# Attention and two mixture layers on one core: a planner's durations, its order, and 30 extra matmuls ahead of the first scores

## The chip, the cores and the metric

One core of a Trainium2 chip runs the whole program. The metric is device time in microseconds (us), median of several runs.

## The reference

Inputs: `q`, `k`, `v` of shape (2, 8, 768, 64), 16 centroids for each head, and the weights of two feed-forward layers. What is computed:

```python
q_assign = argmax(einsum('bhsd,hcd->bhsc', normed(q), normed(centroids)), -1)   # k_assign the same from k
mask = q_assign[:, :, :, None] == k_assign[:, :, None, :]
scores = where(mask, q @ k.T / sqrt(D), -1e9)
x = softmax(scores) @ v                       # (2, 8, 768, 64), then laid out as (1536, 512)
h = x @ w_in;  x = (h * clip(h + 3, 0, 6) / 6) @ w_out          # first layer, 512 -> 2048 -> 512
p = domain_probs / domain_probs.sum(-1)
out = sum(p[:, e] * (relu(x @ w1[e]) @ w2[e]) for e in range(4))  # second layer, 512 -> 1024 -> 512 each
```

## The kernel before, in words

The work is done batch by batch. For batch 0 the program runs attention (`Attn`, its block function is `turned`), then the first layer (`Moe1`), then the second (`Moe2`); attention of batch 1 (block function `block`) is mixed in between the matmuls of batch 0's two layers, and the two layers of batch 1 come last.

Attention goes by pairs of heads (four pairs, `hp`) and blocks of 256 queries (three, `blk`): twelve units in a batch, each of four score tiles (two heads, 128 queries each). `prep` loads the raw heads (`raw`), makes `qa` and `ka` on ScalarE and `kb` and parts of `qa` on VectorE or GpSimd, and gets the cluster of each token: centroid scores on TensorE (`psc`, after the normed centroids were transposed into `cps` and copied to `ct`), a copy `sc`, a transpose `psct`, a chain on VectorE (`mx`, `cs`, `oh` or, for the first pair, `ohq`), and a transpose back (`pso`) that is copied into rows 64 to 80 of `kb` and `qb`. A score tile (`pss`) is two matmul pairs; VectorE takes its maximum (`ut`), ScalarE its exponential (`e`), GpSimd scales it (L752), TensorE transposes it (`pst`), ScalarE or VectorE copies that to `pt`, and the value matmuls (`psv`) follow; ScalarE and VectorE make the float16 halves `x1h` and `x1l` of the result. In batch 1 the transposes are DMAs (`pt<-p`).

While attention of batch 0 runs, `conv_w` turns weights, which are handed in as float64 words, to float32: a load `r64` (a ring of three buffers, L971), ScalarE (L974), GpSimd (L975), three operations on VectorE (L977, L979, L981), a square sum on ScalarE (L983), then two float16 halves that go to DRAM (`hl_i`, `hl_o`) and are read back as `w`. In the layers, products of two float32 matrices are three matmuls of float16 halves (`mm3`, L994 to L996). `post` of `Moe1` takes a finished tile (`psg`): ScalarE (`t`, L1141), VectorE (`t`, L1142), ScalarE and VectorE (`g`, L1143 and L1144). The four tiles of `Moe1`'s first chunk and first token block share one PSUM buffer (L1124), so that each waits for L1142 of the tile before.

No engine's order is written by hand. Every operation is added to an `Order` as a task with an engine, a duration and a priority; `plan` lays the tasks out by list scheduling with these durations, and `emit` issues them in that order. On the chip each engine then works through its own list in order, each instruction waiting on semaphores. The table `PAR` holds the priorities' parameters. The helpers `act`, `dve` and `pool` in `body` turn a tile's width into a duration for the planner; they emit nothing by it.

Of the kernel before, what the change touches and what calls it, by code (L numbers as in the profile page):

```python
# [9 lines left out]
F32 = mybir.dt.float32  # L10
# [4 lines left out]
AF = mybir.ActivationFunctionType  # L15
# [12 lines left out]
def _f32(u):  # L28
# [11 lines left out]
    thr=3060,  # L40
    off=0.0,
    wsl="DD",
    wx=-7.066418236159021,
    wxs=1.7031729906943276,
    wx0=60.44894795273649,
    wl=5.8905461872446105,
    slack=0.05,
    nl=0.5,
    vre=2,
    nbv=12.208119445812287,  # L50
    nbr=19.492100909063655,
    xw=[4.0, 8.0],
    pw=(1, 1),
    prl=10.307879853622739,
    q0=-100.0,
    q1=4.698832831216272,
    psc="ms",
    ql=6,
    ahead=2.5,
    wait=0,  # L60
    wait0=0.8,
    until=15.937819815454496,
    wgap=4,
    ta=23.03227176398944,
    tu=2.65261639137209,
    lead0=24.89126820071733,
    lead2=1.9834016944625252,
    vlead2=-8.255446311119922,
    lead1=2.584304629357875,
    vlead=-26.23423839669475,  # L70
    avp=-2.177772012892397,
    parts=3,
    avpa=-5.181945553955072,
    kn='PPPPPD',
    kt='AAADA',
    kb='DPAD',
    gl=["DDDD", "DDDD"],
    mx=33.765926285870314,
    sp=12.85212467284476,
    spc=-0.7733117880477255,  # L80
    wse=dict(i="P", o="S", **{"1": "P", "2": "A"}),
    v0=49.64382789476431,
    lr=0.3,
    spm=1.5,
    pem=0.0,
    v1=-30.274294106096814,
# [3 lines left out]
    loa="VP",  # L90
    lob="VV",
    r64p=10.082714135814108,
    slow=1.127922433051184,
    psx=3,
    dup=["PSSS", "P"],
    dpx=2,
    trp=5.40052463189909,
    trh=2,
    parta=6,
    cv0=136.29846708597177,  # L100
    cvd=12.748195272086846,
    cva=2,
    cvb=(3, 8, 4),
    wo1=0,
# [4 lines left out]
    wr=8,  # L109
    wob=8,  # L110
    two=[0, 0],
    seq=[0, 1, 3, 2, 5, 4, 6, 7, 9, 10, 8, 11],
    btail=8.42579664942202,
    bu0=37.05195126419793,
    bdu=25.500617255218906,
    bvl=-6.574407994641807,
    bpr=5.123744591407974,
)


# [267 lines left out]
def body(ctx: ExitStack, tc: tile.TileContext, qk, vd, cent, w_in, w_out, probs, w1, w2, out):  # L388
    nc = tc.nc
    B, H, _, S = qk.shape  # L390
# [18 lines left out]
    G = PAR  # L409
    o = Order(tc)  # L410
    add = o.add

    def pe(n, prio, fn, r, w, cols=0):
        return add("PE", n, prio, fn, r, w, cols=cols or 2400 * n)

    def act(n, prio, fn, r, w, ps=False, ap=0, acc=False, tab=None, lag=0.0):
        return add("ACT", 1e-3 * (n * 0.8325 + (93 if ps else 129) + 93 * ap + 93 * acc), prio, fn, r, w, tab=tab, lag=lag)

    def dve(n, prio, fn, r, w, fast=False, ap=False, lag=0.0, lk=False):
        return add("DVE", 1e-3 * (n / (1.92 if fast else 0.96) + 68 + 60 * ap), prio, fn, r, w, lag=lag, lk=lk or fast)  # L420

    def pool(n, prio, fn, r, w, ns=2.1):
        return add("POOL", 1e-3 * (n * ns + 150), prio, fn, r, w, lk=True)

    def dma(nbytes, prio, fn, r, w, lag=0.0, start=0.0):
# [149 lines left out]
    class Attn:  # L575
# [16 lines left out]
        def prep(self, hp, p, lo_eng):  # L592
# [5 lines left out]
            for q in range(2):  # L598
                h = 2 * hp + q
                raw = self.buf("raw", [128, S], F32)  # L600
                dma(393e3, p(0), lambda raw=raw, h=h: nc.sync.dma_start(out=raw.t, in_=qk[b, h]), [], [raw])
                qa, qb, ka, kb = (self.buf(k, [n, S], F32R) for k, n in (("qa", 128), ("qb", 80), ("ka", 128), ("kb", 80)))
                heads.append((qa, qb, ka, kb))
                raws.append(raw)
                act(S, p(1), lambda qa=qa, raw=raw: nc.scalar.activation(out=qa[0:64], in_=raw[0:64], func=AF.Copy, scale=0.125), [raw], [(qa, 0)])
                dma(196e3, p(1), lambda qa=qa, qb=qb: nc.sync.dma_start(out=qb[0:64].bitcast(F32), in_=qa[0:64].bitcast(F32)),
                    [(qa, 0)], [(qb, 0)])

                def low(eng, f, r, w, at=2, n=S):
                    if eng == "V":  # L610
                        dve(n, p(at), lambda: f(nc.vector), r, w, lk=True)
                    else:
                        pool(n, p(at), lambda: f(nc.gpsimd), r, w)

                def keys(qa=qa, ka=ka, kb=kb, raw=raw, after=[sc] if quick and q else [], kl=G["ql"] if quick and q else 0):
                    act(S, p(1), lambda: nc.scalar.activation(out=ka[64:128], in_=raw[64:128], func=AF.Copy), [raw] + after, [(ka, 1)])
# [14 lines left out]
                if quick and q:  # L631
                    late = keys
                else:
                    keys()
# [66 lines left out]

            pe(6 * 0.054, p(5), otr, [oh], [po])
            so = self.buf("so", [64, S], F32R)
            act(S, p(5), lambda: nc.scalar.activation(out=so.t, in_=po.t, func=AF.Identity, scale=ohs.t, bias=ohb.t), [po], [so], ps=True, ap=True)
# [133 lines left out]
        def scores(self, qa, qb, ka, kb, q0, tb, n, p):  # L838
            ps = Buf(p_s[self.b], [128, 2, 512], F32, "pss")

            def score():
# [10 lines left out]
            dve(S, p, lambda: nc.vector.tensor_reduce(out=nb(), in_=ps[:, :, 0:HS], axis=AX.XY, op=ALU.max, negate=True), [ps], [(tb, n)])  # L852
            act(S, p, lambda: nc.scalar.activation(  # L853
                out=e.t.rearrange("p (a b) -> p a b", a=2), in_=ps[:, :, 0:HS], func=AF.Exp, bias=nb(), scale=1.0, accum_out=rs()),
                [ps, (tb, n)], [e, (tb, 2 + n)], ps=True, acc=True, tab=AF.Exp)
            return e

        def sums(self, tb, n, p, unit=1.0 / PSC):
# [552 lines left out]
```

## Time and profile before

| what | value |
|---|---|
| median of 3 runs | 957.32 us (956.35 to 958.79) |
| the profiled execution's own time | 955.95 us |
| its span, first to last instruction | 954.1 us |
| instructions | 16183 |
| TensorE (PE) busy | 918.0 us, 96% of the span |
| VectorE (DVE) busy | 722.6 us, 76% |
| ScalarE (ACT) busy | 648.0 us, 68% |
| GpSimd (POOL) busy | 369.4 us, 39% |

Busy time of an engine is the union of its instructions' times. A matmul's time runs from its first row in to its last row out, and the next one starts before that, so TensorE's share is high even where its pace is not. The 1.85 us between the span and the execution's own time lie outside the instructions.

### The profile page before, as it was taken

The numbers are of one execution on the slowest core, as the hardware profiler recorded it, in microseconds if no ns is written. First come the engines' busy times: TensorE is split into PE (matmuls) and PEld (weight loads), VectorE is DVE, ScalarE is ACT, GpSimd is POOL, SyncE is SP. The second block draws the span as 40 slices with busy tenths as digits, with TensorE's granted clock in tenths as the row PEclk, the third lists the DMA queues.
The fourth block names the chain that finished last, engine by engine and source line by source line (L and its number), as shares of the span: only waits on it lengthen the run. The fifth ranks groups of instructions, "written<-read, shape, count | busy, mean of one in ns | idle before, by whom it ended". The sixth has DMA issues, their size and how long they took to land. (4 is left out here: it accounts for less than half of the span.)

```text
span 954.1 us, 16183 instructions
## 1 busy us (share of the span) xinstructions
PE 918.0 (96%) x5633; PEld 545.6 (57%) x5633; DVE 722.6 (76%) x1513; ACT 648.0 (68%) x1360; POOL 369.4 (39%) x406
## 2 busy tenths in 40 slices
PE   5998998999999998999999999999999999999998
PEld 3776765655555554555565565566655555555553
DVE  8899785887679997798798987855589666564543
ACT  5899986767788787879787754565467654555411
POOL 3566735424535435635455321101132552334100
PEclk9999999999999999999999999999999999999999
DMA  7343339776535475277576677332021221212001
GB/s 228 109 142 98 132 109 323 275 257 218 177 99 180 95 173 150 68 154 167 129 128 145 181 164 219 108 108 91 23 79 46 99 88 46 89 55 79 0 1 67
DMA packets 124369, 121.63 MB, mean 127 GB/s; under 512 B 81472, under 2 KB 81472, under 8 KB 124288
## 3 DMA queue, kind: packets, MB, share of 16 engines
q1 hardware_dynamic: 124288, 120.61, 44.1%
q8 instruction: 44, 0.72, 0.3%
q14 instruction: 37, 0.30, 0.1%
HBM read 81.32 MB, written 14.68 MB: 101 GB/s over the span
## 5 line engine op out<-in xcount | busy, mean ns | idle before, releaser
L900 POOL TENSOR_TENSOR w<-wraw,w 128x512 f16<-128x512 f32 (+1 forms) x128 | 133.9, 1062 | 191.7 <-ACT w L899 147.7
L994 PE MATMUL psm<-w,h 128*128 128x512 f16 x384 | 145.9, 380 | 0.1
L996 PE MATMUL psm<-w,h 128*128 128x512 f16 x384 | 145.5, 379 | 0.0
L995 PE MATMUL psm<-w,h 128*128 128x512 f16 x384 | 145.5, 379 | 0.0
L853 ACT ACTIVATE e<-pss,ut 128x768 f32<-128x768 f32 x96 | 86.6, 903 | 19.2 <-DVE ut L852 14.7
L852 DVE TENSOR_REDUCE ut<-pss 128x1 f32<-128x768 f32 x96 | 91.1, 950 | 8.7 <-PE pss L846 8.1
L1081 ACT ACTIVATE keep<-psw 128x384 f32<-128x384 f32 x96 | 46.6, 487 | 67.9 <-PE psw L1073 67.7
L898 POOL TENSOR_SCALAR wraw<-wraw,wsc 128x512 f32<-128x512 f32 x64 | 47.5, 751 | 94.5 <-DMA wraw<-in_w 43.4
L899 ACT ACTIVATE w<-wraw 128x512 f16<-128x512 f32 (+1 forms) x128 | 72.2, 581 | 17.3 <-POOL wraw L898 6.6
L995 PE MATMUL psg<-g,w 128*128 128x384 f16 x256 | 83.4, 326 | 0.3 <-DVE g L1144 0.3
L994 PE MATMUL psg<-g,w 128*128 128x384 f16 x256 | 83.5, 326 | 0.0
L996 PE MATMUL psg<-g,w 128*128 128x384 f16 x256 | 83.4, 326 | 0.0
L1258 DVE SCALAR_TENSOR_TENSOR oa<-psm,pq,oa 128x512 f32<-128x512 f32 x84 | 61.9, 744 | 22.7 <-PE psm L996 22.5
L995 PEld LDWEIGHTS <-w 128*128 128x128 f16 x512 | 50.1, 98 | 39.2 <-issue 8.1
L996 PEld LDWEIGHTS <-w 128*128 128x128 f16 x512 | 50.0, 98 | 35.6 <-issue 2.5
L994 PEld LDWEIGHTS <-w 128*128 128x128 f16 x512 | 51.0, 100 | 33.9 <-issue 1.4
L1234 DVE SCALAR_TENSOR_TENSOR h<-psw,h 128x384 f16<-128x384 f32 x78 | 43.1, 553 | 31.3 <-ACT h L1233 31.0
L844 PE MATMUL pss<-ka,qa 128*128 128x384 f32 x192 | 61.3, 401 | 4.9 <-ACT e L853 4.5
L1071 PE MATMUL psw<-tx,ws 128*128 128x384 f16 x192 | 62.6, 326 | 1.1 <-DVE h L1234 0.8
L996 PEld LDWEIGHTS <-h 128*128 128x128 f16 x384 | 37.6, 98 | 45.3
L1073 PE MATMUL psw<-tx,ws 128*128 128x384 f16 x192 | 62.6, 326 | 0.0
L1072 PE MATMUL psw<-tx,ws 128*128 128x384 f16 x192 | 62.6, 326 | 0.0
(199 smaller groups left out, 2367.5 us busy)
## 6 DMA issues: line engine op xcount, KB each, us to landing
wraw<-in_w SPq DMA_DIRECT2D x128, 256.0 KB, 3.3
r<-in_w_in SPq DMA_DIRECT2D x16, 512.0 KB, 4.8
r<-in_w_out SPq DMA_DIRECT2D x16, 512.0 KB, 4.9
w<-hl_i SPq DMA_DIRECT2D x32, 256.0 KB, 2.8
w<-hl_o SPq DMA_DIRECT2D x32, 256.0 KB, 4.1
raw<-in_qk SPq DMA_DIRECT2D x16, 384.0 KB, 4.1
vr<-in_vd SPq DMA_DIRECT2D x12, 384.0 KB, 4.9
hl_i<-w SPq DMA_DIRECT2D x16, 256.0 KB, 3.5
```

The source lines that it names most:

```text
L844: nc.tensor.matmul(ps[:, f, 0:HS], qa[:, qs], ka[:, f * HS:f * HS + HS], start=True, stop=False)
L852: dve(S, p, lambda: nc.vector.tensor_reduce(out=nb(), in_=ps[:, :, 0:HS], axis=AX.XY, op=ALU.max, negate=True), [ps], [(tb, n)])
L853: act(S, p, lambda: nc.scalar.activation(out=e.t.rearrange("p (a b) -> p a b", a=2), in_=ps[:, :, 0:HS], func=AF.Exp, bias=nb(), scale=1.0 ...
L899: act(c, p, lambda w=w, raw=raw, c=c: nc.scalar.activation(out=w[:, 0, 0:c], in_=raw[:, 0:c], func=AF.Copy), [raw], [(w, 0)])
L900: pool(c, p, lambda w=w, raw=raw, c=c: nc.gpsimd.tensor_tensor(out=w[:, 1, 0:c], in0=raw[:, 0:c], in1=w[:, 0, 0:c], op=ALU.subtract), [raw ...
L994: nc.tensor.matmul(o_, ah, bh, start=i == 0, stop=False)
L995: nc.tensor.matmul(o_, ah, bl, start=False, stop=False)
L996: nc.tensor.matmul(o_, al, bh, start=False, stop=i == 3)
L1071: nc.tensor.matmul(o_, ah, bh, start=not more and k == 0, stop=False, skip_group_check=more)
L1072: nc.tensor.matmul(o_, ah, bl, start=False, stop=False, skip_group_check=more)
L1073: nc.tensor.matmul(o_, al, bh, start=False, stop=k == 1, skip_group_check=more)
L1258: dve(512, p, lambda: nc.vector.scalar_tensor_tensor(out=oa[:, t], in0=ps.t, scalar=q, in1=oa[:, t], op0=ALU.mult, op1=ALU.add), [ps, qk], ...
```

## The change

Three things change in the file. The planner's duration formulas get other constants (`act`, `dve`, `pool`, and the widths given for a few tasks). The table `PAR` gets other priorities, among them `seq`, the order of the twelve units of batch 0, in which a unit is the number `3 * hp + blk`. And 30 tasks are added for TensorE: a plain matmul of the float32 identity by itself, 128 by 128, into a PSUM tile `spin` that nothing reads.

```diff
-    seq=[0, 1, 3, 2, 5, 4, 6, 7, 9, 10, 8, 11],
+    seq=[1, 0, 3, 2, 5, 4, 6, 7, 9, 10, 11, 8],
...
+    warm=30,
+    wat=2.2,
+    wstep=0.5,
...
-    kn='PPPPPD',
+    kn='PPPPDD',
...
     def act(n, prio, fn, r, w, ps=False, ap=0, acc=False, tab=None, lag=0.0):
-        return add("ACT", 1e-3 * (n * 0.8325 + (93 if ps else 129) + 93 * ap + 93 * acc), prio, fn, r, w, tab=tab, lag=lag)
+        return add("ACT", 1e-3 * (n * 0.8325 + (62 if ps else 104) + 85 * ap + 118 * acc), prio, fn, r, w, tab=tab, lag=lag)
...
-        return add("DVE", 1e-3 * (n / (1.92 if fast else 0.96) + 68 + 60 * ap), prio, fn, r, w, lag=lag, lk=lk or fast)
-
-    def pool(n, prio, fn, r, w, ns=2.1):
+        return add("DVE", 1e-3 * (n / (1.92 if fast else 0.96) + 68 + 60 * ap + 52 * (lk or fast)), prio, fn, r, w, lag=lag, lk=lk or fast)
+
+    def pool(n, prio, fn, r, w, ns=1.92):
...
+    spin = Buf(p_v[0], [128, 128], F32, "spin")
+    for i in range(G["warm"]):
+        w = pe(0.2133, 900.0 if i else -200.0, lambda: nc.tensor.matmul(spin.t, ident.t, ident.t, start=True, stop=True), [], [spin], 512)
+        w.ready = G["wat"] + G["wstep"] * i
```

Engine by engine, the program after holds the same instructions in the same numbers as the program before, and the 30 matmuls; all else is a matter of order. Three places follow, as the two programs list them. In the changed file lines stand three further down (seven further from L1276 on), so L646 of before is L649 of after.

The first place is the head of TensorE's list, from its first matmul to the first transpose of one-hot codes (`ohq`). Before:

```order
L537 MATMUL cps<-ident,scrap 128x128
L646 MATMUL psc<-raw,ct 32x384 x4
L656 MATMUL psct<-ident,sc 128x128 x3
L683 LDWEIGHTS ohq
L683 MATMUL pso<-ident_b,ohq 128x128
```

And after:

```order
L1276 MATMUL spin<-ident 128x128 x5
L540 MATMUL cps<-ident,scrap 128x128
L1276 MATMUL spin<-ident 128x128 x2
L649 MATMUL psc<-raw,ct 32x384 x4
L1276 MATMUL spin<-ident 128x128 x4
L659 MATMUL psct<-ident,sc 128x128 x3
L1276 MATMUL spin<-ident 128x128 x11
L686 LDWEIGHTS ohq
L686 MATMUL pso<-ident_b,ohq 128x128
```

Of the 30 matmuls 22 stand here, around the centroid scores and their transposes; four more stand behind the twelve `pso` transposes, ahead of the first score, and the last four behind the second pair's centroid scores, two score tiles later.

The second place is TensorE's list between the last score tile of the third unit of batch 0 (first row) and that unit's value matmuls (last row); the rows between are later scores (`pss`), transposes (`pst`) and the value matmuls of the unit before. Before:

```order
L846 MATMUL pss<-kb,qb 128x384 x2
L780 MATMUL psv<-pt,vr 64x256 x12
L764 MATMUL pst<-ident,e 128x128 x6
L844 MATMUL pss<-ka,qa 128x384 x2
L846 MATMUL pss<-kb,qb 128x384 x2
L764 MATMUL pst<-ident,e 128x128 x6
...
L846 MATMUL pss<-kb,qb 128x384 x2
L764 MATMUL pst<-ident,e 128x128 x3
L780 MATMUL psv<-pt,vr 64x256 x12
```

And after:

```order
L849 MATMUL pss<-kb,qb 128x384 x2
L767 MATMUL pst<-ident,e 128x128 x3
L847 MATMUL pss<-ka,qa 128x384 x2
L849 MATMUL pss<-kb,qb 128x384 x2
L767 MATMUL pst<-ident,e 128x128 x3
...
L849 MATMUL pss<-kb,qb 128x384 x2
L767 MATMUL pst<-ident,e 128x128 x3
L783 MATMUL psv<-pt,vr 64x256 x12
```

The 12 value matmuls of the unit before no longer stand between, and of `pst` transposes 21 stand there in place of 27; four later score tiles stand there in both, and six small `pso` transposes come in.

The third place is ScalarE's list at the end of attention of batch 0, with buffer numbers: `x1h0` of the last unit, the loads' first step (`wconv<-r64`), and `post`'s first step of the third tile of `Moe1` (`psg1_2039` before, `psg1_2077` after). Before:

```order
L788 ACTIVATE x1h0_602<-psv_1981,vm_66 128x256
L974 ACTIVATE wconv_2049<-r64_1977 128x512
L974 ACTIVATE wconv_2063<-r64_1991 128x512
L1141 ACTIVATE t_2066<-psg1_2039,hlf_76,kt_69 128x384
L1143 ACTIVATE g_2074<-t_2066 128x384
```

And after:

```order
L977 ACTIVATE wconv_2038<-r64_1999 128x512
L791 ACTIVATE x1h0_637<-psv_2015,vm_66 128x256
L986 ACTIVATE scrap_77,am_2023<-wconv_2008 128x512
L1144 ACTIVATE t_2102<-psg1_2077,hlf_76,kt_69 128x384
L977 ACTIVATE wconv_2108<-r64_2036 128x512
```

The first of the two loads' steps now stands ahead of `x1h0`, the second behind the tile's `t`. On the DMA queue the load of `r64_2036` now stands ahead of four read-backs `w<-hl_o`, where its like of before, the next `r64` load, stood behind them.

## Rows read from the trace of the kernel before

**Rows 1.** The page: span, busy time by engine, the granted clock in 40 slices.
```profile
span 954.1 us, 16183 instructions
PE 918.0 (96%) x5633; PEld 545.6 (57%) x5633; DVE 722.6 (76%) x1513; ACT 648.0 (68%) x1360; POOL 369.4 (39%) x406
PEclk9999999999999999999999999999999999999999
```

**Rows 2.** Busy time by stretch: length, each engine, granted clock, DMA share, GB/s.
```profile
0.00:20.00 20.00, 9.20 (x40) 5.86 (x44) 17.07 (x56) 11.78 (x18) 4.69 (x10) 1.00 0.73 220
5.65:38.79 33.14, 25.88 (x151) 18.18 (x152) 30.55 (x68) 24.17 (x48) 15.95 (x16) 1.00 0.67 193
38.79:142.91 104.12, 99.25 (x731) 75.15 (x730) 91.66 (x210) 96.67 (x215) 60.60 (x66) 1.00 0.37 115
142.91:160.00 17.09, 14.24 (x90) 8.58 (x88) 9.13 (x19) 10.95 (x24) 9.76 (x12) 1.00 0.94 329
204.00:220.00 16.00, 13.28 (x81) 7.72 (x80) 14.51 (x33) 13.19 (x27) 4.07 (x6) 1.00 0.77 264
280.00:590.00 310.00, 303.11 (x1939) 176.87 (x1937) 271.04 (x557) 239.06 (x512) 140.77 (x150) 1.00 0.64 152
590.00:720.00 130.00, 128.35 (x784) 76.44 (x783) 89.52 (x185) 73.08 (x140) 24.38 (x24) 1.00 0.27 90
```

**Rows 3.** Groups on TensorE from 0 to 21.9 us: busy, mean ns | idle before.
```profile
L844 PE MATMUL pss<-ka,qa 128*128 128x384 f32 x8 | 3.8, 570 | 1.7 <-ACT e L853 1.7
L656 PE MATMUL psct<-ident,sc 128*128 128x128 f32 x3 | 0.9, 439 | 0.6 <-ACT sc L649 0.6
```

**Rows 4.** The same groups, and two more, from 40 to 140 us.
```profile
L764 PE MATMUL pst<-ident,e 128*128 128x128 f32 x243 | 35.6, 277 | 1.8 <-POOL e L752 1.0 <-DVE pt L773 0.5 <-ACT pt L771 0.2
L780 PE MATMUL psv<-pt,vr 128*64 128x256 f32 x252 | 29.9, 384 | 0.0
L844 PE MATMUL pss<-ka,qa 128*128 128x384 f32 x76 | 22.7, 380 | 2.8 <-ACT e L853 2.6
L656 PE MATMUL psct<-ident,sc 128*128 128x128 f32 x6 | 1.0, 282 | 0.3 <-ACT sc L649 0.3
```

**Rows 5.** Timeline of the head, and a later psc: start, length, [idle before <- releaser].
```profile
5.75 1.63 PE L646 MATMUL psc<-raw,ct 128*32 128x384 f32 x8 [0.73 <-DVE ct L540]
7.98 0.90 PE L656 MATMUL psct<-ident,sc 128*128 128x128 f32 x3 [0.59 <-ACT sc L649]
12.08 1.46 PE L683 MATMUL pso<-ident_b,ohq 128*128 128x128 bf16 x12 [3.20 <-DVE ohq L676]
22.37 0.49 PE L656 MATMUL psct<-ident,sc 128*128 128x128 f32 x3
38.31 0.48 DVE L789 SCALAR_TENSOR_TENSOR x1l<-psv,vm,x1h 128x256 f16<-128x256 f32 x1
68.39 0.85 PE L646 MATMUL psc<-raw,ct 128*32 128x384 f32 x8
```

**Rows 6.** Timeline at the end of batch 0's attention.
```profile
141.91 0.47 ACT L788 ACTIVATE x1h<-psv,vm 128x256 f16<-128x256 f32 x1
142.29 0.66 ACT L974 ACTIVATE wconv<-r 128x512 f32<-128x512 f32 x1
144.93 0.66 ACT L974 ACTIVATE wconv<-r 128x512 f32<-128x512 f32 x1 [1.98 <-DMA r<-in_w_out]
145.49 0.66 ACT L1141 ACTIVATE t<-psg,hlf,kt 128x384 f32<-128x384 f32 x1
146.18 0.55 DVE L1142 SCALAR_TENSOR_TENSOR t<-t,psg 128x384 f32<-128x384 f32 x1 [1.34 <-ACT t L1141]
146.79 0.32 PE L994 MATMUL psg<-x1h,w 128*128 128x384 f16 x1 [2.85 <-DVE t L1142]
```

**Rows 7.** TensorE's waits from 204 to 220 us: total, times, longest.
```profile
PE psg L994 <- DVE t L1142: 2.5, 2, 1.4
```

**Rows 8.** TensorE's waits from 280 to 590 us, the longest three.
```profile
PE psv L826 <- DMA pt<-p: 2.2, 2, 1.4
PE psw L1071 <- DVE h L1234: 1.8, 2, 1.0
PE psm L994 <- DVE h L1234: 0.9, 2, 0.6
```

More of the change, by code (lines that the diff above doesn't have):

```diff
@@ L42 @@
     wsl="DD",
[L43 to L46, printed above, removed]
+    wx=-7.657586520128484,
+    wxs=1.695859560345771,
+    wx0=62.035245197008955,
+    wl=6.318423529745778,
     slack=0.05,
@@ L49 @@
     vre=2,
-    nbv=12.208119445812287,
-    nbr=19.492100909063655,
+    nbv=11.120027900098975,
+    nbr=20.67971033951505,
     xw=[4.0, 8.0],
     pw=(1, 1),
-    prl=10.307879853622739,
+    warm=30,
+    wat=2.2,
+    wstep=0.5,
+    prl=16.802844372814405,
     q0=-100.0,
-    q1=4.698832831216272,
+    q1=2.686101547807026,
     psc="ms",
-    ql=6,
+    ql=4.820226906734026,
     ahead=2.5,
     wait=0,
-    wait0=0.8,
-    until=15.937819815454496,
+    wait0=6.752531767384538,
+    until=16.046857711835983,
     wgap=4,
[L64 to L71, printed above, removed]
+    ta=24.279104197949074,
+    tu=2.7128212897776036,
+    lead0=25.93153280334068,
+    lead2=-1.320707282714463,
+    vlead2=-20.759987884181225,
+    lead1=2.758863465634679,
+    vlead=-24.63396755992383,
+    avp=-4.480475991805788,
     parts=3,
-    avpa=-5.181945553955072,
-    kn='PPPPPD',
+    avpa=-2.719509006977633,
+    kn='PPPPDD',
     kt='AAADA',
@@ L77 @@
     gl=["DDDD", "DDDD"],
-    mx=33.765926285870314,
-    sp=12.85212467284476,
-    spc=-0.7733117880477255,
+    mx=34.64649243705187,
+    sp=12.80211510482788,
+    spc=-3.670489515594658,
     wse=dict(i="P", o="S", **{"1": "P", "2": "A"}),
-    v0=49.64382789476431,
+    v0=38.00468589561768,
     lr=0.3,
@@ L85 @@
     pem=0.0,
-    v1=-30.274294106096814,
+    v1=-18.092676969567798,
     a_pool=dict(raw=2, vr=4, sc=1, so=1, cs=2, oh=3, sm=2, e=7, pt=5, tiny=11, stk=4),
@@ L89 @@
     xbb=1,
-    loa="VP",
+    loa='VP',
     lob="VV",
-    r64p=10.082714135814108,
-    slow=1.127922433051184,
+    r64p=3.4391661879830844,
+    slow=1.1516321961223672,
     psx=3,
@@ L96 @@
     dpx=2,
-    trp=5.40052463189909,
+    trp=7.542615836431141,
     trh=2,
     parta=6,
-    cv0=136.29846708597177,
-    cvd=12.748195272086846,
+    cv0=140.0,
+    cvd=13.09118593581421,
     cva=2,
@@ L111 @@
     two=[0, 0],
-    seq=[0, 1, 3, 2, 5, 4, 6, 7, 9, 10, 8, 11],
[L113 to L117, printed above, removed]
+    seq=[1, 0, 3, 2, 5, 4, 6, 7, 9, 10, 11, 8],
+    btail=7.409152240301774,
+    bu0=30.511495948967404,
+    bdu=25.80889917949137,
+    bvl=-9.279099695049105,
+    bpr=5.179788867014961,
 )
@@ L604, in prep @@
                 raws.append(raw)
-                act(S, p(1), lambda qa=qa, raw=raw: nc.scalar.activation(out=qa[0:64], in_=raw[0:64], func=AF.Copy, scale=0.125), [raw], [(qa, 0)])
+                act(S + 120, p(1), lambda qa=qa, raw=raw: nc.scalar.activation(out=qa[0:64], in_=raw[0:64], func=AF.Copy, scale=0.125), [raw], [(qa, 0)])
                 dma(196e3, p(1), lambda qa=qa, qb=qb: nc.sync.dma_start(out=qb[0:64].bitcast(F32), in_=qa[0:64].bitcast(F32)),
@@ L610, in low @@
                     if eng == "V":
-                        dve(n, p(at), lambda: f(nc.vector), r, w, lk=True)
+                        dve(n + 48, p(at), lambda: f(nc.vector), r, w, lk=True)
                     else:
@@ L615, in keys @@
                 def keys(qa=qa, ka=ka, kb=kb, raw=raw, after=[sc] if quick and q else [], kl=G["ql"] if quick and q else 0):
-                    act(S, p(1), lambda: nc.scalar.activation(out=ka[64:128], in_=raw[64:128], func=AF.Copy), [raw] + after, [(ka, 1)])
+                    act(S + 120, p(1), lambda: nc.scalar.activation(out=ka[64:128], in_=raw[64:128], func=AF.Copy), [raw] + after, [(ka, 1)])
                     d = G["dup"][b][hp % len(G["dup"][b])]
@@ L703, in prep @@
             so = self.buf("so", [64, S], F32R)
-            act(S, p(5), lambda: nc.scalar.activation(out=so.t, in_=po.t, func=AF.Identity, scale=ohs.t, bias=ohb.t), [po], [so], ps=True, ap=True)
+            act(S, p(5), lambda: nc.scalar.activation(out=so.t, in_=po.t, func=AF.Identity, scale=ohs.t, bias=ohb.t), [po], [so], ps=True, ap=2)
             for q in range(2):
@@ L854, in scores @@
                 out=e.t.rearrange("p (a b) -> p a b", a=2), in_=ps[:, :, 0:HS], func=AF.Exp, bias=nb(), scale=1.0, accum_out=rs()),
-                [ps, (tb, n)], [e, (tb, 2 + n)], ps=True, acc=True, tab=AF.Exp)
+                [ps, (tb, n)], [e, (tb, 2 + n)], ps=True, acc=True, ap=0.75, tab=AF.Exp)
             return e
```

## The prediction

> **What bounds the kernel now.** I read the page first, then busy time by stretch, then, inside the stretches where TensorE idles, its waits and the timeline. The page says that TensorE is busy 918.0 of 954.1 us, the next engine 722.6 [rows 1]: 36 us is all that TensorE idles, and only there can a new order gain much. The stretches say where. From 590 us on it idles 1.65 us in 130 [rows 2], so what follows the second attention is a matter of matmuls that the change leaves alone. Up to 590 us four places are left. In the head, to the first `x1l` at 38.79 us [rows 5], TensorE is the idlest of the three big engines: from 5.65 us on it works 25.88 of 33.14 us, VectorE 30.55 [rows 2]. From there to the last `x1l` of batch 0 TensorE works 99.25, ScalarE 96.67 and VectorE 91.66 of 104.12 us; the three are within 8% of each other. At the end of that attention TensorE idles 2.85 us in one piece [rows 6], and 2.72 us between 204 and 220 us [rows 2], 2.5 of them in two waits for `t` [rows 7]. Over the second attention, 280 to 590 us, it idles 6.9 us, in small waits: 2.2 for transposes by DMA, 1.8 and 0.9 for `h` [rows 2, 8].
>
> The clock needs care. The page prints full level in all 40 slices [rows 1], yet up to 21.9 us score matmuls take 570 ns and `psct` transposes 439, where they take 380 and 282 from 40 us on [rows 3, 4]; three `psct` take 0.90 us at 7.98 and 0.49 at 22.37 [rows 5]. So the record does not cover the beginning, and I read the first 22 us as the lower of the two levels (1.2 against 2.4 GHz).
>
> **The change, part by part.** The duration constants emit nothing; they act through the order alone. `kn` is read at an index from 0 to 3, where both strings say P, so it does nothing. No engine gains or loses an instruction but TensorE, so each busy sum stays and only idle time can move.
>
> *The 30 matmuls.* The trace has no plain float32 matmul of 128 columns. Bounds at the low level: a transpose of that size, 0.90/3 = 0.30 us, and a third of the 384-column `psc`, 1.63/3 = 0.54 us; at full level 0.49/3 = 0.16 and 0.85/3 = 0.28 us [rows 5]. All 30 cost 9.0 to 16.3 us at the low level, 4.9 to 8.5 at full, and TensorE idles 20 - 9.20 = 10.8 us in the first 20 [rows 2]. Five stand ahead of `cps`, where nothing waits. Four stand between `psc` and `psct`, where 0.59 us is idle behind `psc`'s modelled end [rows 5]: 0.6 to 1.1 us at full level, which just fits, 1.2 to 2.2 at the low one, which holds `psct` and the VectorE chain behind it up by 0.6 to 1.6 us. Eleven stand ahead of `pso`, where 3.20 us is idle: 1.8 to 3.1 at full level, 3.3 to 5.9 at the low one. What they can give: at full level `psc` ends 0.78 us and `psct` 0.41 us sooner [rows 5]. But their results go to VectorE, which idles only 33.14 - 30.55 = 2.59 us up to the first `x1l` [rows 2]; a result that comes sooner mostly waits for it. Its list shows work of the same amount put ahead of the scores, a `kb` and a `vr` maximum of 0.95 us each, taken from behind them. So the head's change lies between -2.6 and +1.6; I take **-0.7**, a quarter of VectorE's idle time, since the gain must pass through that engine.
>
> The Trainium skill ("TensorE: Matmul & The Clock Gate", Why this matters for your kernels) says that TensorE should be kept busy without a break to have its full clock. By that rule the low-level 9.20 us of the first 20 would shrink by half, 4.6 us; by the rows on VectorE at most 2.6 of it could arrive. The same page (Part 4: PE-mode transpose) says that transposes do not engage the full clock as other matmuls do, which would let the level fall again once these 30 are through. Here the trace disagrees: over 40 to 140 us, with 243 transposes recorded, they average 277 ns against the head's 439 for `psct` [rows 3, 4].
>
> *The rest of batch 0's attention.* Unit order and priorities change, no work. TensorE idles 4.9 us in this stretch, ScalarE 7.5, VectorE 12.5 [rows 2], so -4.9 is the most that a better order gives. Some layer work is also pulled in ahead of the last `x1l` (about one ScalarE and one or two VectorE operations by the lists), which costs there what it saves later. Value matmuls are called for sooner after their scores (the second place in the order); that is a rival below. I take **-0.8**, a sixth of the bound. Starting with block 1 asks for all of `qb` ahead of the first score, two more copies on ScalarE; VectorE's two copies into `kb` stand in the same gap, so I cost it at nothing, and at half a microsecond if they are done early.
>
> *The end of that attention.* Here a step can be followed. ScalarE's `wconv` of 144.93 us waits 1.98 us for a load; `t`, behind it in the list, starts at 145.49, VectorE's `t` at 146.18, and TensorE, whose tile needs the one PSUM buffer, at 146.79 after 2.85 us [rows 6]. After the change the tile's `t` has ahead of it one load step, `x1h` and a square sum, and the second load step stands behind it. If the first load has landed, `x1h` runs at 141.91 as before, the square sum (some 0.8 us with its read-out, an estimate from the 0.66 of its neighbours) ends near 143.5, the tile itself is done near 143.8, `t` takes 0.66 and 0.55 us with some 0.1 to hand over each: TensorE goes on at about 145.2 in place of 146.79. Gain 1.6, less 0.1 for the tile's end: **-1.5**. What is late next is the second load step, and behind it `g` and the fourth tile's `t`; but the tile after that has other buffers, so nothing on TensorE waits at once. That load now stands ahead of four read-backs on the DMA queue, needed only by the second product. Bounds: -2.85, and +1.4 if the first load lands as late as the one that ScalarE waited for (144.9): then `x1h` starts 3 us later, `t` at about 146.9 and TensorE at 148.2.
>
> *204 to 220 us.* The lists keep the same shape: load steps and four conversions ahead of two `t`. I take **0**, bounds -2.5 and +2.
>
> *Second attention.* Scores and value matmuls are moved among the layer's matmuls; by the lists the TensorE work between a unit's last score and its first value matmul is 0.3 us longer on the mean of twelve units, with the shortest unchanged. TensorE idles 6.9 us; I take **-1.5**, the larger part of the waits for DMA transposes [rows 8], with -5 and +4 as bounds. From 590 us on: 0.
>
> Sum: -0.7 - 0.8 - 1.5 + 0 - 1.5 = -4.5. Against the profiled execution's 955.95 that is 951.45; the median stands 1.37 higher, so **952.8 us**, 0.47% below 957.32. About 0.3%, 2.9 us, is what a measurement of this kernel can tell from no change. The likeliest case's own range is 949 to 954.4.
>
> **The rivals.**
> *Nothing to be told.* The head is VectorE's, and each stall removed appears at the next wait in the list (the second load's step behind `t`). Only the third term then arrives, and other waits eat half of it: 956.5. For it: three engines within 8% of each other over 104 us [rows 2]. Against: one wait of 2.85 us has a named cause that the new order takes away.
>
> *Slower: value matmuls called for too soon.* In the second place in the order, twelve value matmuls (24 records at 29.9/252 = 0.12, 2.8 us) and six transposes (35.6/243 = 0.15 each, 0.9 us) [rows 4] no longer stand between the third unit's last score and its value matmuls; with what comes in, these are 3 us nearer, and by the same count over all twelve units some 10 us. TensorE's list is in order, so a `psv` that waits for its `pt` copy holds the scores behind it, and with them VectorE and ScalarE. Before, `psv` waited 0.0 us [rows 4], so there is slack of unknown size. If half of the 10 us exceeds it: +4.8, and if what this wait holds up also eats the other terms, 962. It decides from where the copies end later than some 8 us after the last score; against it, ScalarE's copies come early in its list too.
>
> *Slower: the clock stays low under the 30.* Then 16.3 - 10.8 = 5.5 us do not fit, and the four ahead of `psct` and eleven ahead of `pso` hold up the chain: 957.3 + 5.5 - 2 for the later terms = 961. Against: from 4.6 us on TensorE's list has hardly a break.
>
> *The clock bounds the head.* Half of 9.20 us comes through, and the other terms hold: 957.3 - 4.6 - 3.8 = 949. Named above is the page that asks for it. Against: VectorE's 2.59 us.
>
> **How the numbers follow.** Forecast 0.46; nothing to be told 0.28; value matmuls too soon 0.15; clock low under the 30, 0.05; clock bounds the head 0.06. Faster by over 0.3%: 0.46 + 0.06 = 0.52; slower: 0.20; within: 0.28. The range for 8 in 10 goes from 947.5, where the head and the second attention give a good part of their bounds, to 961, which leaves out the worse half of the slower cases.
>
> **What would show it.** In the profile after: `psct` near 0.5 us for three by its first run, and VectorE still busy over nine tenths from 6 us to the first `x1l`, that within 1 us of 38.8; a wait of TensorE for `t` near the last `x1l` of about 1.4 in place of 2.85; waits for `pt<-p` in the second attention below 2.2; nothing new after 590. I would be wrong if `psv` shows waits in the first attention, if the last `x1l` of batch 0 comes more than 2 us later or 4 us earlier, or if `x1h` stands behind a load.

## The result, and the profile after

The changed kernel takes 968.98 us (median of 4 runs, 966.85 to 971.08) against 956.87 for the kernel before in the same runs: a ratio of 1.0119, 95% interval 1.0103 to 1.0135. It is slower by 1.2%, where 0.5% faster was forecast; the range (947.5 to 961) does not hold it. The profiled run took 971.08 us, its span 968.9, against 954.1 [rows 1]. It is the slowest of the four, and the profiled execution of the kernel before (955.95) was faster than any of the timed ones beside it (956.35 to 958.79). So the two traces are some 15 us apart where the medians are 12.1, and what is read from them below adds up to some 3 us too much.

The page of the changed kernel:

```profile
span 968.9 us, 16296 instructions
...
PE 927.8 (96%) x5693; PEld 553.0 (57%) x5693; DVE 730.5 (75%) x1513; ACT 649.6 (67%) x1360; POOL 366.3 (38%) x406
...
PEclk9999999999997999999999999999999999999999
```

TensorE is busy 9.8 us more than before (the 30 new matmuls, and some at the lower level), and idle 41.1 in place of 36.1 us. The clock has a dent in the 13th slice, 291 to 315 us. Busy time by stretch, as in [rows 2] (the ends of the batches moved a little; the second attention now ends near 606 us):

```profile
0.00:20.00 20.00, 15.18 (x100) 11.85 (x100) 16.58 (x54) 11.45 (x17) 4.70 (x10) 1.00 0.67 207
5.65:38.46 32.81, 27.36 (x200) 20.70 (x200) 30.88 (x68) 24.36 (x49) 15.76 (x16) 1.00 0.60 184
38.46:142.72 104.26, 100.66 (x731) 76.15 (x730) 92.93 (x213) 97.76 (x217) 60.98 (x68) 1.00 0.42 124
142.72:160.00 17.28, 15.93 (x100) 9.62 (x99) 7.26 (x17) 12.00 (x25) 9.52 (x12) 1.00 1.00 363
...
204.00:220.00 16.00, 11.63 (x72) 6.67 (x72) 15.49 (x36) 13.01 (x28) 4.00 (x6) 1.00 0.72 229
...
280.00:606.00 326.00, 308.75 (x1947) 178.90 (x1946) 277.75 (x562) 239.93 (x513) 141.91 (x151) 0.98 0.61 145
606.00:736.00 130.00, 128.93 (x790) 77.00 (x789) 91.05 (x187) 73.44 (x140) 23.30 (x25) 1.00 0.27 91
```

The second attention (sixth row) takes 326 us with 17.25 idle on TensorE, where it took 310 with 6.9. Everything else is within 2 to 3 us of before. To place the loss more closely I summed TensorE's matmuls in order, each at its full-level price and without the identity ones, and compared the times at which the two traces reach the same sum. The changed kernel's lag:

| time before, us | 161 | 246 | 289 | 310 | 526 | 569 | end |
|---|---|---|---|---|---|---|---|
| lag, us | -1.75 | +1.3 | +0.45 | +11.4 | +16.3 | +16.0 | +15.0 |

With other prices for the same matmuls (their mean times, or their columns) the points at 289 and 310 us move by up to 1 us, the others hardly. So it is ahead after the first attention, gives that back at 190 to 215 us, and loses 10 to 11 us in one place. TensorE's waits in the whole kernel, the longest:

```profile
PE psam L556 <- DVE am L554: 6.8, 1, 6.8
PE psg L997 <- DVE t L1145: 6.5, 3, 3.3
...
PE psc L649 <- ACT e L856: 2.0, 1, 2.0
```

The first is the new one. The timeline of the changed kernel shows what stands around it, all engines, at 292 to 306 us:

```profile
292.09 0.49 ACT L652 ACTIVATE sc<-psc 128x384 f32<-128x384 f32 x1
...
293.92 0.95 DVE L721 TENSOR_REDUCE am<-vr 128x1 f32<-128x768 f32 x1
...
294.78 0.74 DVE L1259 TENSOR_SCALAR oa<-psm,pq 128x512 f32<-128x512 f32 x1
...
295.44 0.94 DVE L721 TENSOR_REDUCE am<-vr 128x1 f32<-128x768 f32 x1
...
295.67 0.52 PE L659 MATMUL psct<-ident,sc 128*128 128x128 f32 x3 [1.20 <-ACT h L1236]
...
301.43 0.94 DVE L721 TENSOR_REDUCE am<-vr 128x1 f32<-128x768 f32 x1
...
302.29 0.54 DVE L679 TENSOR_TENSOR oh<-cs,mx 128x384 bf16<-128x384 f32 x1
...
302.75 0.14 DVE L554 TENSOR_REDUCE am<-am 128x1 f32<-128x4 f32 x1
...
302.95 0.37 PE L556 MATMUL psam<-ident,am 128*1 128x128 f32 x1 [6.76 <-DVE am L554]
...
303.95 0.54 DVE L1237 SCALAR_TENSOR_TENSOR h<-psm,h 128x384 f16<-128x384 f32 x1
...
304.59 0.85 PE L703 MATMUL pso<-ident_b,oh 128*64 128x128 bf16 x6
...
304.95 0.53 DVE L1237 SCALAR_TENSOR_TENSOR h<-psm,h 128x384 f16<-128x384 f32 x1
...
305.67 0.53 PE L998 MATMUL psm<-x2l,w 128*128 128x384 f16 x1
...
305.99 0.53 PE L999 MATMUL psm<-x2h,w 128*128 128x384 f16 x1
```

The same place in the kernel before:

```profile
291.62 0.52 PE L656 MATMUL psct<-ident,sc 128*128 128x128 f32 x3 [0.28 <-DVE oa L1256]
291.97 0.33 PE L994 MATMUL psm<-x2h,w 128*128 128x384 f16 x1
292.13 0.33 PE L995 MATMUL psm<-x2l,w 128*128 128x384 f16 x1
...
297.87 0.54 DVE L676 TENSOR_TENSOR oh<-cs,mx 128x384 bf16<-128x384 f32 x1
...
298.84 0.33 PE L996 MATMUL psm<-x2h,w 128*128 128x384 f16 x1
299.10 0.52 PE L700 MATMUL pso<-ident_b,oh 128*64 128x128 bf16 x6
...
303.00 0.14 DVE L551 TENSOR_REDUCE am<-am 128x1 f32<-128x4 f32 x1
...
305.73 0.27 PE L553 MATMUL psam<-ident,am 128*1 128x128 f32 x1
```

And the engines over the two 10 us, first the kernel before, then the changed one:

```profile
290.00:300.00 10.00, 9.72 (x62) 5.52 (x61) 9.90 (x19) 9.74 (x25) 5.99 (x6) 1.00 0.67 218
300.00:310.00 10.00, 9.68 (x54) 5.71 (x53) 8.75 (x24) 6.69 (x16) 7.61 (x10) 1.00 0.52 166
290.00:300.00 10.00, 4.99 (x31) 2.57 (x27) 9.88 (x15) 9.80 (x23) 4.29 (x5) 0.93 0.80 243
300.00:310.00 10.00, 6.29 (x30) 3.66 (x30) 9.54 (x30) 5.63 (x13) 1.71 (x2) 0.56 0.54 156
```

On TensorE of the changed kernel `psct` (the centroid scores of batch 1's first pair, turned) is followed at once by `psam` and `psbc` (the maximum of batch 1's values, across partitions and back) and `pso` (the routing codes, turned). All three need VectorE, which is full: 9.88 us of the 10 up to 300. In the kernel before VectorE is as full (9.90), but `psct` starts at 291.62 us and `pso` at 299.10, and 14 blocks of three `psm` matmuls (the products of the second layer) stand between them, 13 of 384 columns and one of 512; `psam` comes later and waits for nothing. TensorE's waits at 295 to 304 us are 1.20 (`psct`), 6.76 (`psam`) and 0.76 us (`psbc`), 8.7 of the 10 to 11 us together. One more thing is seen in the last two rows of the changed kernel: `psm` takes 0.53 us and the next starts 0.32 behind it, twice the 0.16 between the first two `psm` of the kernel before. The clock's records give the lower level from 298.56 to 308.80 us, after TensorE had stood since 296.2, and again for 3.4 us from 523.84, after the wait of 2.0 us for `e`.

### The profile page after: what moved, and what is told of

The parts are those of the page before. It is cut to its first block, busy times and chain, and to the rows that moved or that the text cites. A ratio compares the mean times of both kernels' runs of the same rounds, so it can differ in the third digit from the quotient of the medians.

```text
span 968.9 us, 16296 instructions
## 1 busy us (share of the span) xinstructions
PE 927.8 (96%) x5693; PEld 553.0 (57%) x5693; DVE 730.5 (75%) x1513; ACT 649.6 (67%) x1360; POOL 366.3 (38%) x406
## 5 line engine op out<-in xcount | busy, mean ns | idle before, releaser
L901 POOL TENSOR_SCALAR wraw<-wraw,wsc 128x512 f32<-128x512 f32 x64 | 45.0, 712 | 108.5 <-DMA wraw<-in_w 30.4
L999 PEld LDWEIGHTS <-h 128*128 128x128 f16 x384 | 37.6, 98 | 45.5 <-issue 0.3
L997 PEld LDWEIGHTS <-h 128*128 128x128 f16 x384 | 38.0, 99 | 43.4 <-issue 5.7
```

The lines of the kernel that those rows point to most:

```text
L997: nc.tensor.matmul(o_, ah, bh, start=i == 0, stop=False)
L999: nc.tensor.matmul(o_, al, bh, start=False, stop=i == 3)
```

## The experiments

All were timed in 4 to 12 runs beside the kernel before. A is the changed kernel, B the one before (the "theory A" and "theory B" of the first two expectations are not these). What was expected of each stands quoted behind its edit.

| kernel | median us | ratio to B | 95% interval |
|---|---|---|---|
| A | 968.98 | 1.0119 | 1.0103 to 1.0135 |
| TensorE's order alone (1) | 973.52 | 1.0162 | 1.0139 to 1.0184 |
| that and two `h` (2) | 969.14 | 1.0116 | 1.0096 to 1.0136 |
| 28 matmuls in the wait (3) | 967.32 | 1.0107 | 1.0083 to 1.0130 |
| one number back (4) | 977.00 | 1.0197 | 1.0175 to 1.0218 |
| A to 160 us, then B (5) | 954.66 | 0.9967 | 0.9955 to 0.9980 |
| B to 280 us, then A (6) | 972.56 | 1.0152 | 1.0136 to 1.0167 |
| B with the 30 matmuls (7) | 957.69 | 1.0009 | 0.9988 to 1.0029 |
| A without them (8) | 970.51 | 1.0131 | 1.0112 to 1.0150 |
| VectorE's order too (9) | 970.29 | 1.0133 | 1.0119 to 1.0147 |
| B to 308 us, then A (10) | 967.29 | 1.0104 | 1.0090 to 1.0117 |
| new durations only (11) | 978.36 | 1.0213 | 1.0199 to 1.0227 |
| new table only (12) | 974.38 | 1.0181 | 1.0162 to 1.0200 |
| cover and chain first (13) | 972.06 | 1.0144 | 1.0116 to 1.0171 |
| that and `so` (14) | 972.28 | 1.0161 | 1.0147 to 1.0176 |
| that and `psn` (15) | 968.80 | 1.0119 | 1.0096 to 1.0142 |
| A to 280 us, then B (16) | 959.85 | 1.0026 | 1.0011 to 1.0040 |

The runs 1, 2, 9 and 13 to 15 move planned entries by hand before they are emitted; the numbers are those of the entries, and every engine keeps its own order but for them.

**Is the wait for `psam` the loss?**

```
(1) + o.move([([1749, 1750, 1751, 1752], "behind", 1742),    # 12 psm behind VectorE's first h
    +         ([2814, 2815], "behind", 1752)])               # psam and the maximum behind it
(2) + o.move([([1742], "ahead of", 2806), ([1748], "behind", 2838),   # the two h, ahead of am, behind mx
    +         ([1749, 1750, 1751, 1752, 1755, 1756, 1757, 1758], "behind", 1748)])
```

Expected of (1):

> The order of the changed kernel, but on TensorE the next twelve psm matmuls (one block of four groups, 12 x 0.16 = 2.0 us) stand ahead of psam and psbc at 296-304 us; VectorE's list is the same but for the maximum behind psam, which now stands behind one h. Theory A (psam and psbc alone hold TensorE up): the twelve run in the wait from 296.2 us, psam then waits about 4.7 us instead of 6.8, and the time is 966 to 967 against 968.98. Theory B (the two PSUM tiles of psm are both still held, because the two h of VectorE that read them, 303.95 and 304.95, stand behind four maxima of the values on VectorE): the wait of some 7 us is only renamed, now psm behind h, and the time is 969 to 971.

Expected of (2):

> As the first, and besides VectorE's two h stand ahead of the maxima (as soon as ScalarE has written their first half, 293.7 and 295.6 us), and 24 psm matmuls (3.9 us) stand ahead of psam. Theory B: TensorE goes on behind psct, psam's wait falls to some 3 to 4 us, the clock's fall is shorter or gone, and the time is 962 to 965.5. Theory A expects no more here than for the matmuls themselves, and the same or better from the order of TensorE alone. If the loss lies in the rest of the second attention, whatever is done here comes back later: 967 to 970.

The first run's waits, TensorE:

```profile
PE psm L1020 <- DVE h L1260: 8.3, 2, 8.2
```

The wait has only got another name, as theory B said: the two PSUM tiles of `psm` were held by the two `h`. The time, 973.52, lies above both of the expected ranges. Theory A, which was my first reading of the row, is out. But the second run did not give what B promised either (969.14, expected 962 to 965.5): the 24 matmuls ran at 296 to 300 us, `psam` waited 3.2, and then the first scores waited 2.5 us for their copies; the lag at 310 us was 12.1.

**The clock's share.**

```
(3) + busy = Buf(p_v[1], [128, 128], F32, "busy")
    + t = pe(0, 0, lambda: [nc.tensor.matmul(busy.t, ident.t, ident.t, ...) for _ in range(28)], [], [busy])
    + o.seq.insert(o.seq.index(("task", o.tasks[2814])), ("task", t))
```

Expected of (3):

> The changed kernel with 28 more matmuls of the identity (unread, some 0.21 us each, 6.0 us) right ahead of psam, where TensorE now waits 6.8 us. The wait itself can't get shorter. If the fall of the clock (298.6 to 308.8 us at half) is caused by that wait and costs what the rows show (some eleven psm 0.32 us apart instead of 0.16, and the six pso), the granted clock stays full there and the time is 966.5 to 967.5. If the fall comes from something else, or the work behind waits for VectorE anyway: 968.5 to 970.

The 28 took 6.42 us and `psam` waited 0.52. In the profiled run the lower level then covered 307.30 to 310.71 us instead of 10.24 us. The median came down by 1.7 us, inside the expected range, but the intervals of the two ratios overlap. The two runs whose clock stayed full took 966.54 and 966.62 us, 2.4 less than A's median. So the clock's fall is a small part of the 12 us, some 2 us; the rest is there at full level too.

**One number back.**

```
(4) - v1=-18.092676969567798,
    + v1=-30.274294106096814,
```

Expected of (4):

> The changed kernel with one number of its table as before (v1 back from -18.09 to -30.27, so batch 1's maxima are due 12 us later), planned anew. If the early due time is what costs the 12 us at 293-312 us: the wait of psam is under 1 us, and the time 956 to 960. If VectorE has that much work around there in any order of these durations, the loss only moves to later places in the second attention: 965 to 970.

Slower still. The wait for `psam` went and the stretch at 289 to 310 us lost about 4 us, but 331 to 399 us lost another 12 to 14, to waits of `pss` and `psw` and a clock at the lower level. 977.00 is above both expected ranges. That the early due time alone makes the loss is out; that any plan with these durations has it somewhere is not shown by one.

**Which stretch of the order.** For these the planned lists were cut and joined, with no new plan: first all that one plan starts before the seam, then the rest in the other's order. In short (the programs hold the joined list as numbers):

```
  + o.follow([x for x in plan_a if x.start < 160.0] + [x for x in plan_b if x not in first])   # (5); (16): 280.0
  + o.follow([x for x in plan_b if x.start < 280.0] + [x for x in plan_a if x not in first])   # (6); (10): 308.0
```

Expected of (5):

> A splice of the two orders, nothing planned anew: every instruction that the changed kernel's plan starts in its first 160 us stands in the changed kernel's order (the matmuls of the identity, the head, batch 0's attention), everything else behind it in the order of the kernel before. By the two traces the changed kernel is 1.75 us ahead at equal work of TensorE at that place. If the gain there is real and the loss lies only in what follows: 955 to 956.3 against a median of 957.7 for the kernel before. If the first part leaves work undone that falls due later: 957.5 or more.

Expected of (6):

> The splice the other way: the order of the kernel before for what its plan starts in its first 280 us, then the changed kernel's order for all the rest; no matmuls of the identity. If the loss of 14.6 us that the traces show behind 290 us belongs to the order there (second attention), whatever came ahead: 970 to 973. If it needs what the changed order did or left undone before 280 us (the loads, the transforms that VectorE had still to do): 957 to 964.

Expected of (10):

> The order of the kernel before for what its plan starts in its first 308 us (past psam, psbc and the first scores of batch 1), then the changed kernel's order; no matmuls of the identity. If 11.8 of the loss are made between 290 and 312 us by the order in that stretch and the other 3 us behind it by the order there: 960 to 962.5. If the stretch only shows first what the whole second attention costs in the new order: 967 to 973.

Expected of (16):

> The splice with a later seam: everything that the changed kernel's plan starts in its first 280 us in its order, the rest in the order of the kernel before. By the traces the changed kernel is 0.45 us behind at 287 us. If the loss is made by the order behind 280 us alone: 957 to 959.5, within 0.3% of the kernel before. If the changed order of 160 to 280 us had left the second attention something to catch up (ScalarE's sc is 3.5 us later in it): 962 to 970.

The first splice is faster than both kernels: with the head and the first attention in the changed order the time is 0.33% lower (0.20 to 0.45). Its one trace does not show all of that: it is 1.5 us ahead of B's at 161 to 345 us, loses 3 between there and 430, and ends level with it (spans 954.1 both); it is the slowest of the six runs of (5), beside the fast one of B. The second has the whole loss though all of its first 280 us are B's; its wait for `psam` was 9.7 us:

```profile
PE psam L714 <- DVE am L712: 9.7, 1, 9.7
```

The splice of A to 280 us and then B lost 1 us at 289 to 299 and is 0.26% slower than B (4 us of its loss lie near 430 us, 3.8 at 190 to 215). So the order behind 280 us makes the loss; what came before it adds a few us at most. This also answers whether A's VectorE merely came late to the place: by 290 us it had worked 232.71 us against B's 235.41, but in (16) it had worked 233.20, and TensorE was busy 38.23 of the next 40 us all the same. The seam at 308 us tells less than I wanted: all went as in B up to 312 us, and then two later scores waited 3.1 and 2.1 us for `e` and the clock was at the lower level from 319.32 to 329.56 us; the lag rose by 8 to 9 us up to 331. My reading, not tested, is that the matmuls that stand between the scores in A's list had been spent in B's part. 967.29 lies at the edge of the rival's range.

**The 30 matmuls.**

```
(7)   B's order + the 30 ahead of the same instructions as in A
(8)   A's order - the 30
```

Expected of (7):

> The kernel before, its order to the last instruction, with the 30 matmuls of the identity ahead of the same TensorE instructions as in the changed kernel (5 ahead of cps, 2 of psc, 4 of psct, 11 of the transposes of ohq, 4 and 4 later). The clock is then full from some 8 us instead of 22 us, but TensorE waits for VectorE for most of the head: 956.5 to 958 (a change of under 1 us either way). If the clock bounds the head: 953 to 955.

Expected of (8):

> The changed kernel, its order to the last instruction, without the 30 matmuls of the identity. The clock is then at half until some 22 us. If VectorE bounds the head: 968.5 to 970 against 968.98. If the clock bounds it: 971 to 973.

By their medians neither can be told from its base, which rules out the 4.6 us of a head bounded by the clock; 1 or 2 us either way are not ruled out. Single traces differ by as much: in (7)'s the first `x1l` ends at 41.66 us against 38.79 in B's, with the lower level from 20.72 to 27.55, and three of its 12 runs took 963 to 964 us, where B's beside them took 955.7 to 960.6 (one of 3352.78, far out, aside); in (8)'s it ends at 39.52 against 38.46 in A's, with the full level from 24.55 us only.

**The halves of the change.**

```
(11)  durations of A and warm=30, table otherwise as in B, planned anew
(12)  durations of B, table of A, planned anew, without the 30
```

Expected of (11):

> One half of the change: the new durations (ScalarE, VectorE, GpSimd) and the 30 matmuls of the identity, with all other numbers of the table as before, planned anew. If the new numbers of the table make the costly second attention, this is near the kernel before: 955 to 960. If the new durations alone order it anew for the worse: 963 to 972.

Expected of (12):

> The other half: the new numbers of the table with the durations as before and without the matmuls of the identity, planned anew. If the new numbers alone make the costly second attention: 965 to 975. If it takes both halves together: 956 to 961.

Either half alone is slower than both together, and in other places: at 160 us of B they already lag by 12.2 and 9.1 us. So (11), above both of its ranges, and (12), inside its first one, do not tell which half makes the second attention slow. With A and (4) that makes four orders planned anew, each 1.2 to 2.1% slower than B.

**What would close the hole.**

```
(9)  (2) + ([1726, 1731], "ahead of", 2824), ([1736], "behind", 2834),    # the three oa sooner
           ([2843], "ahead of", 2814)                                     # pso ahead of psam
(13) as (9), and psct and its mx, cs, mx, oh as soon as sc is there; 11 blocks of psm between psct and pso,
           six psm up to psam, two blocks up to psbc, two behind it; psam, psbc in psv's PSUM buffer
(14) (13) + so ahead of what stood before it on ScalarE, its transfers, four blocks ahead of psam
(15) (14) + psn and its steps behind pso's block; the first ut behind vm's first step, the first e ahead of vh
```

Expected of (9):

> The changed kernel with VectorE's list at 288-304 us put more as in the kernel before: two oa stand in VectorE's gap of 1.5 us ahead of qa (288 us), the third behind the second kb, the two h ahead of the first and behind the second maximum; on TensorE 24 psm matmuls and pso stand ahead of psam. Theory: VectorE hands PSUM back too late there (oa 294.8 to 299.5 us, h 303.95 and 304.95), and with the order alone the waits of psct and of the first scores of batch 1 behind it (1.7 and 2.5 us in the run that moved only the h) go, while psam's 3 us stay: 963.5 to 966.5. Rival: VectorE has 9.9 of 10 us of work there in whatever order, and TensorE waits as long elsewhere: 968 to 970.

Expected of (13):

> The changed kernel with the order at 286-318 us made by hand after a pattern of the kernel before: psct of batch 1's first pair and its chain on VectorE and GpSimd (mx, cs, the second mx, oh) as soon as ScalarE's sc is there (292.6 us), 11 blocks of three psm matmuls (5.4 us) between psct and pso, six more with the later products and another four blocks between pso, psam, psbc and the first scores; psam and psbc write psv's PSUM buffer. Theory: the loss is the cover that is missing, since nothing stands between psct and psam, psbc and pso in the changed order, while in the kernel before 13 blocks of three matmuls do: psct some 2.5 to 3 us sooner, no wait over 1.5 us up to the first scores, 958.5 to 963. Rival: VectorE is full there and TensorE has spent its other work too early, so the waits come back at the scores behind it: 966 to 970.

Expected of (14):

> As the one before, and besides ScalarE's so (which stood at 307.2 us, behind a tx that waited for VectorE, though pso was done at 300.5 us) comes as soon as pso is there, its four transfers stand ahead of the next load of values, and psam stands behind four more blocks of psm, the first scores between psam and psbc. Theory (missing cover, and a chain held up at each of its in-order steps): first scores at 305 to 306.5 us instead of 310.1, psam's wait under 2 us, time 965 to 968.5. Rival (what is gained here is lost at the scores behind it, since their cover is spent): first scores sooner, but 969 to 972.

Expected of (15):

> As the one before, and besides psn (the norm of the next weights) stands right behind pso's block of matmuls on TensorE, its two steps on VectorE behind it, and the first scores' maximum (ut) and exponent (e) come ahead of the kt, vl and vh that stood before them. The wait of 6.0 us at the second scores (306 to 314 us: e behind a weight's conversion, behind GpSimd's wraw, behind wv, behind psn) should go, the second scores come at 308.5 to 310 us, and the time is 965.5 to 968.5 if the cover still to be had behind it carries TensorE. If that cover is spent (seven blocks that stood between the later scores now stand ahead of the first): waits of 2 us and more at the scores from 310 to 330 us, 969 to 972.

Each run took away much of the wait that it aimed at, and each found the next. None reached the time that its theory gave: (9), (13) and (14) came out above their rivals' ranges, by 2 us at most, and (15) between its two. In (9) the two `oa` did not fill VectorE's gap, since they waited for TensorE until 289.80 us; `pso` waited 3.3 us for `oh` and the scores 2.7 for their copies. In (13) `psam` still waited 3.3 us; `pso` came at 300.02 us, 4.6 sooner, but its reader stood behind a `tx` on ScalarE:

```profile
300.02 0.52 PE L726 MATMUL pso<-ident_b,oh 128*64 128x128 bf16 x6
...
306.77 0.52 ACT L1052 ACTIVATE tx<-keep 128x384 f16<-128x384 f32 x1 [1.19 <-DVE keep L1040]
307.20 0.97 ACT L730 ACTIVATE so<-pso,ohb,ohs 64x768 fp32r<-64x768 bf16 x1
```

In (14) `so` ran at 300.63 and the first scores at 305.29 us, 4.8 sooner; the second scores then waited for the first `e`, which stood behind a weight, behind GpSimd, which had waited for `psn`'s chain:

```profile
311.45 0.55 POOL L596 TENSOR_TENSOR wv<-wv,half 128x1 f32<-128x1 f32 x1 [9.05 <-DVE wv L595]
...
313.03 0.42 ACT L925 ACTIVATE w<-wraw 128x256 f16<-128x256 f32 x1 [3.11 <-POOL wraw L924]
...
314.38 1.01 PE L870 MATMUL pss<-ka,qa 128*128 128x384 f32 x2 [5.99 <-ACT e L879]
```

In (15) that wait was 0.9 us, and the third scores waited 3.1. Busy time of TensorE and VectorE over 290 to 330 us, from the windows of each:

| | B | A | (2) | (9) | (13) | (14) | (15) | (16) | (5) |
|---|---|---|---|---|---|---|---|---|---|
| TensorE, of 40 us | 39.11 | 31.28 | 31.80 | 31.76 | 31.00 | 29.91 | 32.06 | 38.23 | 39.20 |
| VectorE, of 40 us | 38.41 | 36.26 | 34.94 | 35.01 | 35.10 | 34.60 | 38.27 | 38.44 | 38.38 |

The five arrangements by hand ((2), (9), (13), (14), (15)) leave TensorE at 30 to 32 us; B's order gives 38 to 39, whether A's first 160 or 280 us stand ahead of it. My theory that the missing cover between `psct` and `pso` is the loss did not hold as a cure: cover moved there was missing at the scores behind it. In (15) VectorE is as busy as in B and TensorE is not.

## Why the prediction was wrong

The step that failed is the term for the second attention, "I take **-1.5**", with bounds of -5 and +4: by the traces it was +14.6 (lag 0.45 at 289 us, 15.0 at the end), 10 to 11 of them at 289 to 310 us, where TensorE waited 8.7 us at `psct`, `psam` and `psbc` and then ran at the lower level up to 308.80. Runs (6) and (16) put the loss in the order behind 280 us. I had sized it by what TensorE idles there in the kernel before, 6.9 us [rows 2], and by one count in the new order, matmuls between a unit's last score and its first value matmul. I did not read the place where attention's preparation meets the layer's matmuls, where `psam`, `psbc` and `pso` now stand behind `psct` with nothing between, each needing VectorE, which was full there in the kernel before as well (9.90 of 10 us at 290 to 300). No rival had this mechanism, and the bound of +4 rested on no row of it. That the new order puts these three behind `psct` stood in the list, and that VectorE is full there in the windows of before; that this would cost 10 us did not stand anywhere. Some 5 us more of lag came between 310 and 526 us in smaller pieces, the longest a wait of 2.0 us at 521; these were not followed.

The other steps, one by one:
- "the low-level 9.20 us" and the head's **-0.7**: `psct` took 0.49 us for three, as foreseen, yet began at 8.83 in place of 7.98, held up by the matmuls ahead of it; the transposes of `ohq` began at 13.72 in place of 12.08 and the first score at 15.26 in place of 13.30. So the earlier `psct` did not come; a delay did, near the 0.6 to 1.6 us that the prediction had for the lower level, though the level was full from 8.43 us. Still the first `x1l` ended at 38.46, 0.3 sooner, with VectorE busy 30.88 of 32.81 us: that VectorE bounds the head fits, how the term came about was not foreseen. The rival "the clock stays low under the 30" is out by the record of this profile, "the clock bounds the head" by the medians of (7) and (8). That the level would not fall again once the 30 are through holds for this profile and not for all: it was the lower one from 14.36 to 17.77 us in that of (2), which has the same order up to there, and from 20.72 to 27.55 in that of (7).
- The rest of batch 0's attention, **-0.8**: about +0.1; the last `x1l` ended at 142.72 us, 0.2 sooner in all.
- The end of that attention, **-1.5**, from 146.79 to "about 145.2": it came as worked out.

```profile
143.73 0.67 ACT L1144 ACTIVATE t<-psg,hlf,kt 128x384 f32<-128x384 f32 x1 [0.59 <-PE psg L999]
...
144.43 0.56 DVE L1145 SCALAR_TENSOR_TENSOR t<-t,psg 128x384 f32<-128x384 f32 x1 [0.16 <-ACT t L1144]
...
145.04 0.32 PE L997 MATMUL psg<-x1h,w 128*128 128x384 f16 x1 [1.35 <-DVE t L1145]
```

  1.35 us are left of 2.85 [rows 6]. Run (5), which keeps this and the head and leaves out the rest, shows the three terms together as a real gain: forecast -3.0, measured 0.33% or 3.2 us (1.9 to 4.3) below B. That the two agree is in part luck: by the traces of A and (5) the lead at 161 us is 1.75 and 1.5 us, nearly all of it this one term, and where the rest of the 3.2 comes from stays open.
- 204 to 220 us, **0**: it lost. TensorE's waits for `t` are 1.82 us at 195.7 and 3.29 at 211.5, 5.1 together against 2.5 [rows 7], and its busy time from 204 to 220 us fell from 13.28 to 11.63 of 16. From 181 to 246 us the lag rose by 3.1. In the stretch itself that is 1.65 us more of idle time, inside the bound of +2, but the step reaches ahead of 204 us, and as a whole it cost more than the bound.
- Rival "value matmuls called for too soon": no wait of `psv` for `pt` in the first attention, 0.6 us in the second, against 2.2 [rows 8]. So that rival did not happen; that part of the **-1.5** came, and was lost many times over.
- "Nothing new after 590": the lag does not rise after 606 us; TensorE idles 1.07 of 130 us there.

What stays open: which few entries of B's order behind 280 us make it hold together. Moving up to 48 entries of A's by hand did not find them.

## What to carry to other kernels

Where every engine runs a list in order and the tightest is 96% busy, a table planned anew was here a new draw for each place where lists meet, not a shift of the old times (four of four came out slower). Read in both orders what covers each round trip from TensorE to another engine and back, and check that engine's free time there, before pricing a stretch by its idle time. The engine that a long wait names may only be the last of several, so put one other instruction in its place before mending it. When a new order is better in one stretch and worse in another, a splice of the two, cut where both have done the same work, tells which and may keep the gain.

## What the runs showed of the hardware

I had not expected the clock to fall in mid-kernel. After TensorE had stood from 296.2 us its level was the lower one from 298.56 to 308.80 us, and after a wait of 2.0 us (521.0 to 523.0 us) from 523.84 to 527.25, while a longer wait (3.29 us, up to 211.5 us) left no such record in this profile. In others with the same order there it did: in that of (8), after a wait of 3.30 us up to 212.49, the level was the lower one from 212.28 to 215.69. So the same wait need not have the same effect twice. With 28 unread matmuls in the first wait the record shrank to 3.41 us, and two of that kernel's runs had a granted clock of 1.0, at 966.54 and 966.62 us. In the head the record has the full level from 8.43 us with the 30 matmuls, against 21.96 before, and this was worth nothing that the medians could tell; in run (7), with the same matmuls, it fell again from 20.72 to 27.55 us. Three `psct` took 0.49 us at 8.83 us, and 0.90 at 7.98 in the kernel before [rows 5].
